# Transposes and first keys as full-array products, an unstrided gate product, and new planner durations in an attention-plus-GLU kernel

## The chip, the cores and the metric

The kernel runs on one core of one Trainium2 chip. The metric is the device time of the whole program in microseconds, the median of several runs. The program before takes 753.09 us (three runs, 751.25 to 753.7).

## What is computed

One sequence of 2048 tokens of width 512 goes through two branches that share their input, and a per-token gate mixes the two results. All inputs are bf16.

```python
# x: [1, 2048, 512]; 32 heads of width 16; F = 1376
def _A_ref(x, wqkv, wo):
    qkv = transpose((x @ wqkv).reshape(B, S, 3, H, Dh), 2, 0, 3, 1, 4)
    q, k, v = qkv[0], qkv[1], qkv[2]
    scores = einsum("bhqd,bhkd->bhqk", q, k) * (Dh ** -0.5)
    p = softmax(scores, axis=-1)
    o = einsum("bhqk,bhkd->bhqd", p, v)
    return transpose(o, 0, 2, 1, 3).reshape(B, S, D) @ wo

def _B_ref(x, w_gate, w_up, w_down):
    return ((x @ w_gate) * (x @ w_up)) @ w_down

g = sigmoid((x * gate_w).sum(-1, keepdims=True))
out = g * _A_ref(A_x, A_wqkv, A_wo) + (1 - g) * _B_ref(A_x, ...)
```

## The kernel before

**Tiles.** x is kept transposed: `xT(kt, lo, hi)` is the 128 features of tile `kt` by the tokens lo to hi. The 2048 tokens are four chunks of 512. A score block is 128 keys by 512 queries of one head: one bank of PSUM (128 x 512 f32). There are 32 rounds `m` (four query chunks, four groups of eight heads, two halves of a group), and each round has 16 key tiles by four heads, so 64 blocks a round and 2048 in all. The array is used as two row groups of 64 rows by four column groups of 32: a "pack" is four matmuls of 64x32 weights and 512 moving columns on one row group, and packs on row groups 0 and 1 run at the same time. In the planner these are the resources `pe0` and `pe1`.

**Exponentials.** Most blocks go from PSUM through ScalarE (ACT, line 1284, two banks to an instruction as a rule) into cells of the tile `PT`. About 550 blocks go through VectorE instead (line 1348): the score is turned into the bits of a bf16, and three shifted copies of it are made (line 1300 on GpSimd, line 1301 on VectorE), which are multiplied with four scaled versions of V (line 728 makes those). So a block of ACT costs one cell and one set of weighted sums, and one of VectorE four.

**Weighted sums.** `pv_pack` (line 1635) multiplies cells with V, whose tiles have a column of ones for the denominators. The last round (m = 31) uses all 128 rows for a product, and forms its denominators with a second product (line 1646). Normalising goes over DMAs (`den`, `rscr`, `rb`), in the last round over ACT (lines 1873 and 1874), then come the last products (lines 1858 and 1882) and the output.

**Fills.** Everything else that TensorE does is a "fill" that the planner puts between score and sum packs: transposing x (`mk_x`, line 580: products of pieces of x with an identity), q, k and v (`mk_q`, `mk_k`, `mk_v`), the gate logits (`mk_gate`, line 764), the GLU (`mk_ug`, `mk_d`) and the output projection (`mk_wo`). All but x and the gate go through `tile4` (line 544). A fill that is not `wide` does its packs on one row group and then the other half of its rows on the other; a `wide` one takes both row groups at once. Each fill has a bank, which VectorE (ACT for two pieces of the first chunk) copies out: line 606 for x, 622 for keys, 738 for v, 679 for q. ACT makes the first q itself, masked, in two instructions (line 697).

**Order.** Nothing is scheduled on the chip. While the program is built, an event-driven planner runs through the whole kernel with assumed durations and writes down for each engine a fixed order, with semaphore waits between engines; an engine then works its list in order, so that an instruction that has to wait holds up all that stands behind it in that list. The assumed durations and policy are the constants at the head of `_build`:

- `PEC` a pack, `PEL` the time until its result can be used, `PSW` a change between the two array shapes, `LEAD`; `a_cad`, `A_LAT`, `d_cad`, `D_LAT`, `p_cad`, `P_LAT` the same for ACT, VectorE and GpSimd
- `PH`: before this time, packs are taken to last twice as long
- `NF0`, `NF`: how many fills may be open at a time, before and after the first `U0` score blocks
- `KF`: how many of the upper four banks a score block for VectorE leaves free while no fill is open
- `WIDE0`: which of the first fills are wide (before: none)

Scores for ACT use banks 0 to 3, all else banks 4 to 7. Score packs come first in `pe_policy`, then sums and fills. At the start x arrives by DMA in five pieces (line 427), followed by weights.

Of the kernel before, what the change touches and what calls it, by code (L numbers as in the profile page):

```python
# [179 lines left out]
def _build(nc, A_x, A_wqkv, A_wo, W_gate, W_up, W_down, gate_w, out):  # L180
# [25 lines left out]
    NH = 2  # L206
    VT = 33 * H // 2
    INF = 1e9
    PEC, PSW, PEL, LEAD = 0.2165, 0.108, 0.41, 0.05
    DTH = 1.2  # L210
    CQ = 3
    VN = 1000
# [8 lines left out]
    AHEAD = 80  # L221
    LOOK = 200
    NF = 1
    NF0 = 3
    U0 = 100
    PB = 4
    PH = 10.5
    VD = 11
    CD = 6
    PL = 8  # L230
# [3 lines left out]
    AB = 4  # L234
    DB = 4
    BURST = 0
    WIDE0 = False
    AW = 0.2
    KF = 1

    def a_cad(n):
        return 0.053 + 0.4267 * n

    A_LAT = 0.17

    def d_cad(n):
        return 0.068 + n / 960.0
# [1 line left out]
    def d_fast(n):  # L249
        return 0.068 + n / 3840.0  # L250

    D_LAT = 0.12

    def p_cad(n):
        return 0.157 + n / 1200.0

    P_LAT = 0.1

    x2 = A_x.rearrange("b s d -> (b s) d")
    out2 = out.rearrange("b s d -> (b s) d")  # L260
# [2 lines left out]
    with ExitStack() as stack:  # L263
# [170 lines left out]
        def xn(ch, tt):  # L434
            return PT[:, xs_first[ch] + tt, :].bitcast(BF16)
# [102 lines left out]
        }  # L538

        def tile4(pe, r, bank, w, lhs, rhs, s0, s1):  # L540
            o = None
            q = slice(0, 128) if r is None else slice(64 * r, 64 * r + 64)
            for i in range((w + 31) // 32):
                o = pe.matmul(  # L544
                    ps[32 * i : min(w, 32 * i + 32), bank, :],
                    lhs(32 * i, min(w, 32 * i + 32))[q],
                    rhs[q],
                    start=s0,
                    stop=s1,
                    tile_position=(64 * (r or 0), 32 * i),  # L550
                    skip_group_check=True,
                )
            return o
# [20 lines left out]
        def mk_x(ch, kt):  # L574
            def pk(pe, bank, rg, s0, s1):
                o_ = None
                q = slice(64 * rg, 64 * rg + 64)
                for tt in range(4):
                    for i in range(4):
                        o_ = pe.matmul(  # L580
                            ps[32 * i : 32 * i + 32, bank, tt * 128 + 64 * rg : tt * 128 + 64 * rg + 64],
                            xn(ch, tt)[q, kt * 128 + 32 * i : kt * 128 + 32 * i + 32],
                            idt[q, q],
                            start=True,
                            stop=True,
                            tile_position=(64 * rg, 32 * i),
                            skip_group_check=True,
                        )
                return o_

            def evac(bank, last):
                def after(o):
                    ev_x[ch, kt] = o
                    release(banks[bank], [o])
                    done_with(("xn", ch), last)

                if ch == 0 and kt % 2:
                    aq_small.append(
                        (0.48, [last], lambda a: a.activation(xT(kt, 0, 512), ps[:, bank, :], ACT.Identity), after)
                    )  # L600
                    return
                dve_job(
                    0,
                    d_cad(512),
                    lambda: [last],
                    lambda v: v.tensor_copy(xT(kt, ch * 512, (ch + 1) * 512), ps[:, bank, :]),  # L606
                    after,
                )

            return _Fill("x", [pk], lambda: d_xn[ch] + [o_id], evac, 0)  # L610

        def mk_k(b, ch):
            def evac(bank, last):
# [144 lines left out]
        def mk_gate():  # L758
            def pk(kt):
                def f(pe, bank, rg, s0, s1):  # L760
                    o_ = None
                    q = slice(64 * rg, 64 * rg + 64)
                    for ch in range(NCH):
                        o_ = pe.matmul(  # L764
                            ps[32 * ch : 32 * ch + 32, bank, :],
                            gwr[q, kt, :],
                            xT(kt, ch * 512, (ch + 1) * 512)[q].rearrange("q (t p) -> q p t", p=128),
                            start=s0,
                            stop=s1,
                            tile_position=(64 * rg, 32 * ch),  # L770
                            skip_group_check=True,
                        )
                    return o_

                return f

            def evac(bank, last):
# [21 lines left out]
                            allow_slow_non_contiguous=True,  # L799
                        )  # L800

                dve_job(2, d_cad(512), lambda: [last], lambda v: v.tensor_copy(grow, ps[:, bank, :]), after)

            def gate2(e1):
                def a1(e2):
# [893 lines left out]
        def fill_issue(t, fu, r, deps):  # L1699
# [3 lines left out]
            g = f.packs[f.pos % n]  # L1703
            own = []
            if f.wide:
                d = to_wide() + {"gate": 0.5, "x": 0.07}.get(f.name, PEC)
                s0, s1 = f.pos == 0, f.pos == n - 1
                o = issue_pe(t, (0, 1), d, PEL - PEC, lambda pe: g(pe, bank, None, s0, s1), deps, "pe_f")
                tot = n
            else:  # L1710
                if f.pos == n:
                    own = [f.last]
                s0, s1 = f.pos == 0, f.pos == 2 * n - 1
                o = issue_pe(t, (r,), to_small() + PEC, PEL - PEC, lambda pe: g(pe, bank, r, s0, s1), deps, "pe_f", own)
                tot = 2 * n
# [217 lines left out]
```

## Time and profile before

| | |
|---|---|
| runs, median (lowest, highest) | 753.09 us (751.25, 753.7) |
| the profiled execution | 751.66 us |
| its span, first to last instruction | 749.8 us |
| TensorE (PE) busy, instructions | 731.3 us, 22327 matmuls |
| ScalarE (ACT) busy | 706.2 us |
| VectorE (DVE) busy | 646.7 us |
| GpSimd (POOL) busy | 505.6 us |
| mean granted TensorE clock | 0.985 |

A matmul's end is modelled and matmuls overlap, so that PE busy at 98% does not mean that the array is at its limit; the other engines' times are measured. "PEld" is the loading of weights, which runs ahead of the matmuls. The time of an instruction on ACT or VectorE overlaps a little with that of the next. "issue" as the reason of idle time means that the profile shows nothing that the engine waited for.

### The profile page before, as it was taken

The numbers are of one execution on the slowest core, as the hardware profiler recorded it, in microseconds if no ns is written. First come the engines' busy times: TensorE is split into PE (matmuls) and PEld (weight loads), VectorE is DVE, ScalarE is ACT, GpSimd is POOL, SyncE is SP. The second block draws the span as 40 slices with busy tenths as digits, with TensorE's granted clock in tenths as the row PEclk, the third lists the DMA queues.
The fourth block names the chain that finished last, engine by engine and source line by source line (L and its number), as shares of the span: only waits on it lengthen the run. The fifth ranks groups of instructions, "written<-read, shape, count | busy, mean of one in ns | idle before, by whom it ended". The sixth has DMA issues, their size and how long they took to land.

```text
span 749.8 us, 49215 instructions
## 1 busy us (share of the span) xinstructions
PE 731.3 (98%) x22327; PEld 367.9 (49%) x22328; DVE 646.7 (86%) x1266; ACT 706.2 (94%) x764; POOL 505.6 (67%) x549
## 2 busy tenths in 40 slices
PE   6999999999999999999999999999999999999996
PEld 4554454555444555545455544445545554444432
DVE  3576599999989999989989988998999888999975
ACT  3699699999998999999999999999999999999985
POOL 1135486878675877878778786786777658585752
PEclk7699999999999999999999999999999999999999
DMA  8200012122005121110512111014221200010100
GB/s 248 65 9 5 9 34 56 43 60 59 9 13 123 39 68 51 52 29 10 118 37 65 51 58 37 16 36 98 55 47 58 65 14 23 8 30 4 28 11 30
DMA packets 77633, 35.01 MB, mean 47 GB/s; under 512 B 60784, under 2 KB 74480, under 8 KB 77424
## 3 DMA queue, kind: packets, MB, share of 16 engines
q1 hardware_dynamic: 76624, 31.47, 17.1%
q8 instruction: 175, 2.87, 1.6%
q10 hardware_dynamic: 800, 0.39, 0.2%
q14 instruction: 34, 0.28, 0.1%
HBM read 25.23 MB, written 2.35 MB: 37 GB/s over the span
## 4 chain that ended last, share of the span: by engine, by line
PE 95%; DMA 1%; DVE 1%; issue 1%; ACT 0%; SPq 0%
PE ps L1635 37%; PE ps L1189 33%; PE ps L544 22%; PE ps L580 1%; PE ps L764 1%; PE ps L1646 1%; DMA PT<-in_B_w_down_dram 1%; DMA PT<-in_A_x_dram 0%; DVE PT L1348 0%; DMA PT<-in_B_w_up_dram 0%; SPq L416 0%; DVE ost L1891 0%; DVE PT L606 0%; ACT rb L1874 0%; PE ps L1882 0%
## 5 line engine op out<-in xcount | busy, mean ns | idle before, releaser
L1284 ACT ACTIVATE PT<-ps 128x1024 bf16<-128x1024 f32 (+1 forms) x750 | 700.4, 1037 | 24.5 <-PE ps L1189 16.6
L1300 POOL TENSOR_SCALAR PT<-PT 128x1024 int16<-128x1024 int16 (+1 forms) x500 | 470.0, 968 | 175.1 <-DVE PT L1301 141.8
L1635 PE MATMUL ps<-PT,VV 64*32 64x512 bf16 (+1 forms) x7275 | 547.0, 377 | 1.5 <-issue 0.3
L1189 PE MATMUL ps<-QT,KT 64*32 64x512 bf16 x8192 | 481.8, 381 | 1.1 <-issue 1.0
L544 PE MATMUL ps<-PT 64*32 64x512 bf16 x5696 | 411.4, 383 | 4.5 <-issue 2.2
L1348 DVE TENSOR_SCALAR PT<-ps 128x512 int16<-128x512 f32 x530 | 358.4, 704 | 50.2 <-PE ps L1189 42.0
L1635 PEld LDWEIGHTS ps<-PT,VV 64*32 64x32 bf16 (+1 forms) x7275 | 179.1, 92 | 126.4 <-PE ps L1635 42.0
L1189 PEld LDWEIGHTS ps<-QT,KT 64*32 64x32 bf16 x8192 | 138.0, 89 | 167.4 <-ACT PT L1284 97.1
L544 PEld LDWEIGHTS ps<-PT 64*32 64x32 bf16 x5696 | 139.0, 92 | 57.4 <-PE ps L544 9.9
L1301 DVE TENSOR_SCALAR PT<-PT 128x1024 int16<-128x1024 int16 (+1 forms) x442 | 152.0, 409 | 0.5
L728 POOL TENSOR_SCALAR VV<-VV 128x528 bf16<-128x528 bf16 x20 | 12.6, 635 | 46.9 <-DVE VV L728 42.8
L544 PE MATMUL ps<-wo,OT 64*32 64x512 bf16 x480 | 36.2, 378 | 0.1
L897 DVE CAST usb<-ps 128x512 bf16<-128x512 f32 (+1 forms) x44 | 30.0, 681 | 1.4 <-PE ps L544 1.4
L912 DVE TENSOR_TENSOR PT<-ps,usb 128x512 bf16<-128x512 f32 (+1 forms) x44 | 29.8, 679 | 1.0 <-PE ps L544 1.0
L1544 POOL TENSOR_TENSOR OT<-oraw,rb 128x512 bf16<-128x512 f32 x16 | 20.5, 1280 | 6.3 <-DMA rb<-rscr 3.5
L1566 DVE COPY oraw<-ps 128x512 f32<-128x512 f32 x31 | 21.2, 684 | 1.0 <-PE ps L1635 0.8
L622 DVE CAST KT<-ps 128x512 bf16<-128x512 f32 x16 | 11.6, 727 | 9.1 <-PE ps L544 8.9
L738 DVE CAST VV<-ps 128x512 bf16<-128x512 f32 x16 | 10.9, 690 | 8.5 <-PE ps L544 8.5
L606 DVE CAST PT<-ps 128x512 bf16<-128x512 f32 x14 | 9.1, 686 | 9.0 <-PE ps L580 9.0
L544 PEld LDWEIGHTS ps<-wo,OT 64*32 64x32 bf16 x480 | 11.5, 91 | 6.7 <-PE ps L544 1.6
L961 DVE TENSOR_SCALAR bsb<-ps,omg 128x512 bf16<-128x512 f32 x16 | 11.8, 738 | 3.2 <-PE ps L544 3.2
L580 PE MATMUL ps<-idt,PT 64*32 64x64 bf16 x512 | 10.5, 220 | 4.0 <-issue 2.2
(45 smaller groups left out, 97.5 us busy)
## 6 DMA issues: line engine op xcount, KB each, us to landing
PT<-in_B_w_up_dram SPq DMA_DIRECT2D x40, 128.0 KB, 3.1
PT<-in_B_w_gate_dram SPq DMA_DIRECT2D x40, 128.0 KB, 3.1
PT<-in_B_w_down_dram SPq DMA_DIRECT2D x20, 256.0 KB, 2.9
rb<-rscr SPq DMA_DIRECT2D x15, 256.0 KB
out_dram<-ost SPq DMA_DIRECT2D x16, 128.0 KB, 1.9
QT<-QR SPq DMA_DIRECT2D x124, 16.0 KB, 2.0
oraw<-oraw SPq DMA_DIRECT2D x60, 32.0 KB, 2.1
PT<-in_A_x_dram SPq DMA_DIRECT2D x3, 512.0 KB, 9.0
```

Of the source, the lines that this page charges most:

```text
L544: o = pe.matmul(ps[32 * i : min(w, 32 * i + 32), bank, :], lhs(32 * i, min(w, 32 * i + 32))[q], rhs[q], start=s0, stop=s1, tile_position=( ...
L580: o_ = pe.matmul(ps[32 * i : 32 * i + 32, bank, tt * 128 + 64 * rg : tt * 128 + 64 * rg + 64], xn(ch, tt)[q, kt * 128 + 32 * i : kt * 128 ...
L897: lambda v: v.tensor_copy(usb[0:w, n % 2, :], ps[0:w, bank, :]),
L912: lambda v: v.tensor_tensor(hT[0:w, f, :], ps[0:w, bank, :], usb[0:w, n % 2, :], ALU.mult),
L1189: o_ = pe.matmul(ps[32 * i_ : 32 * i_ + 32, x, :], KT[64 * r : 64 * r + 64, b, kt * 128 + 32 * i_ : kt * 128 + 32 * i_ + 32], QT[64 * r : ...
L1284: lambda a: a.activation(span(PT, cs).bitcast(BF16), span(ps, bs), ACT.Exp, scale=ESC),
L1300: return lambda e: e.tensor_scalar(span(PT, ds), span(PT, cs), 1.0, float(SH[k]), ALU.mult, ALU.add)
L1301: return lambda e: e.tensor_single_scalar(span(PT, ds), span(PT, cs), float(SH[k]), ALU.add)
L1348: lambda v: v.tensor_scalar(span(PT, cs), span(ps, bs), IOFF, 0.0, ALU.add, ALU.max),
L1544: lambda g: g.tensor_tensor(OT[:, pair % 6, :], oraw[:, 0, :], rb[:, :], ALU.mult),
L1566: lambda v: v.tensor_copy(oraw[:, p, :], ps[:, bank, :]),
L1635: o_ = pe.matmul(ps[32 * j : 32 * j + 32, ob, :], v_ap(k, kt, 8 * b + 2 * j + p, p)[rows], PT[rows, cell, :].bitcast(BF16), start=f0, stop ...
```

## The change

Six things are edited; the order of all work is planned anew with them.

1. x is transposed with full-array products: four of 128x128 for a piece (`mk_x`) in place of 32 of 64x64, with `wide=True`.
2. `WIDE0` goes from `False` to `"k"`: the first four key products (`mk_k(0, ch)`) are wide, and `tile4` makes one 128x128 by 512 product where it made four of 32 columns on each row group.
3. The gate product reads x in its stored order; the copy out of PSUM (line 802) does the reordering that the product's strided read did.
4. The planner's durations change; the last line gives a wide transposition `XC` in place of 0.07.
5. `PH` goes from 10.5 to 0, so that no packs are planned at double length.
6. `NF0` goes from 3 to 2 and `KF` from 1 to 0.

```diff
-    PEC, PSW, PEL, LEAD = 0.2165, 0.108, 0.41, 0.05
+    PEC, PSW, PEL, LEAD = 0.2155, 0.13, 0.437, 0.05
...
-    NF0 = 3
+    NF0 = 2
...
-    PH = 10.5
+    PH = 0.0
...
-    WIDE0 = False
+    WIDE0 = "k"
+    XC = 0.26
     AW = 0.2
-    KF = 1
+    KF = 0
 
     def a_cad(n):
-        return 0.053 + 0.4267 * n
+        return 0.058 + 0.4267 * n
...
-    D_LAT = 0.12
+    D_LAT = 0.15
...
-    P_LAT = 0.1
+    P_LAT = 0.12
...
         def tile4(pe, r, bank, w, lhs, rhs, s0, s1):
+            if r is None:
+                return pe.matmul(ps[0:w, bank, :], lhs(0, w), rhs, start=s0, stop=s1, skip_group_check=True)
             o = None
-            q = slice(0, 128) if r is None else slice(64 * r, 64 * r + 64)
+            q = slice(64 * r, 64 * r + 64)
...
         def mk_x(ch, kt):
             def pk(pe, bank, rg, s0, s1):
                 o_ = None
-                q = slice(64 * rg, 64 * rg + 64)
                 for tt in range(4):
-                    for i in range(4):
-                        o_ = pe.matmul(
-                            ps[32 * i : 32 * i + 32, bank, tt * 128 + 64 * rg : tt * 128 + 64 * rg + 64],
-                            xn(ch, tt)[q, kt * 128 + 32 * i : kt * 128 + 32 * i + 32],
-                            idt[q, q],
-                            start=True,
-                            stop=True,
-                            tile_position=(64 * rg, 32 * i),
-                            skip_group_check=True,
-                        )
+                    o_ = pe.matmul(
+                        ps[:, bank, tt * 128 : tt * 128 + 128],
+                        xn(ch, tt)[:, kt * 128 : kt * 128 + 128],
+                        idt[:],
+                        start=True,
+                        stop=True,
+                        skip_group_check=True,
+                    )
                 return o_
...
-            return _Fill("x", [pk], lambda: d_xn[ch] + [o_id], evac, 0)
+            return _Fill("x", [pk], lambda: d_xn[ch] + [o_id], evac, 0, wide=True)
...
                             gwr[q, kt, :],
-                            xT(kt, ch * 512, (ch + 1) * 512)[q].rearrange("q (t p) -> q p t", p=128),
+                            xT(kt, ch * 512, (ch + 1) * 512)[q],
...
-                dve_job(2, d_cad(512), lambda: [last], lambda v: v.tensor_copy(grow, ps[:, bank, :]), after)
+                dve_job(2, d_cad(512), lambda: [last], lambda v: v.tensor_copy(grow.rearrange("q (p t) -> q p t", t=4), ps[:, bank, :].rearrange("q (t p) -> q p t", p=128)), after)
...
         for f_ in fills:
-            f_.wide = f_.wide or WIDE0
+            f_.wide = f_.wide or f_.name in WIDE0
...
-                d = to_wide() + {"gate": 0.5, "x": 0.07}.get(f.name, PEC)
+                d = to_wide() + (XC if f.name == "x" else PEC)
```

More of the change, by code (lines that the diff above doesn't have):

```diff
@@ L549, in tile4 @@
                     stop=s1,
-                    tile_position=(64 * (r or 0), 32 * i),
+                    tile_position=(64 * r, 32 * i),
                     skip_group_check=True,
```

## The prediction

> **What bounds the kernel now.** I read the page first, then the busy time by stage, then the list of ACT in order of time wherever a stage showed ACT idle.
>
> ```profile
> span 749.8 us, 49215 instructions
> PEclk7699999999999999999999999999999999999999
> L1284 ACT ACTIVATE PT<-ps 128x1024 bf16<-128x1024 f32 (+1 forms) x750 | 700.4, 1037 | 24.5 <-PE ps L1189 16.6
> ```
>
> ```profile
> core 0: us, PE busy (x) PEld busy (x) DVE busy (x) ACT busy (x) POOL busy (x), PEclk, DMA share, GB/s
> 0.00:31.89 31.89, 23.93 (x792) 14.95 (x800) 13.12 (x28) 12.74 (x15) 2.73 (x12) 0.68 0.69 183
> 31.89:75.00 43.11, 42.86 (x1433) 22.59 (x1424) 30.21 (x65) 42.80 (x47) 18.82 (x27) 1.00 0.03 6
> 75.00:86.00 11.00, 11.00 (x144) 4.85 (x128) 3.66 (x6) 5.46 (x5) 3.00 (x2) 1.00 0.01 1
> 86.00:225.00 139.00, 138.21 (x4397) 70.89 (x4398) 127.64 (x248) 137.67 (x150) 106.08 (x115) 1.00 0.16 38
> 225.00:250.00 25.00, 23.59 (x756) 11.55 (x744) 23.56 (x49) 22.97 (x26) 16.41 (x18) 1.00 0.46 97
> 250.00:715.00 465.00, 463.42 (x14316) 232.97 (x14320) 427.71 (x833) 462.13 (x497) 344.66 (x363) 1.00 0.18 44
> 715.00:749.80 34.80, 28.26 (x541) 10.11 (x530) 20.82 (x41) 22.42 (x30) 13.87 (x16) 0.97 0.07 21
> ```
>
> Length less ACT's busy time gives ACT's idle by stage: 19.15, 0.31, 5.54, 1.33, 2.03, 2.87 and 12.38 us, 43.6 in all. Where the bulk of the blocks is worked, ACT is idle under 1% of the time, so the exponentials set the pace: the span is ACT's busy time, 706.2, plus these 43.6. PE's 98% in the page is overlap of modelled ends. The change is therefore priced by what it does to ACT's work and to its three large idle stages: the head, the gate at 75 to 86 us, and the tail.
>
> **The head: what ACT waits for.** ACT in order of time:
>
> ```profile
> 12.39 1.27 ACT L697 ACTIVATE QT<-ps,mask 128x512 bf16<-128x512 f32 x2 [5.16 <-PE ps L544]
> 14.67 1.94 ACT L1284 ACTIVATE PT<-ps 128x1536 bf16<-128x1536 f32 x2 [1.01 <-PE ps L1189]
> 19.23 1.94 ACT L1284 ACTIVATE PT<-ps 128x1024 bf16<-128x1024 f32 x2 [2.62 <-PE ps L1189]
> 23.62 1.02 ACT L1284 ACTIVATE PT<-ps 128x1024 bf16<-128x1024 f32 x1 [2.46 <-PE ps L1189]
> 31.89 28.79 ACT L1284 ACTIVATE PT<-ps 128x1024 bf16<-128x1024 f32 x31 [0.31 <-PE ps L1189]
> ```
>
> The first block goes to ACT at 14.67 and ACT is full only from 31.89. TensorE's weight loads and windows of that time tell why:
>
> ```profile
> 11.93 0.12 PEld L544 LDWEIGHTS ps<-PT 64*32 64x32 bf16 x9 [2.03 <-issue]
> 17.14 0.71 PEld L580 LDWEIGHTS ps<-idt,PT 64*32 64x32 bf16 x58 [2.37 <-issue]
> 21.42 0.10 PEld L544 LDWEIGHTS ps<-PT 64*32 64x32 bf16 x2 [1.87 <-issue]
> ```
>
> ```profile
> 0.90:11.90 11.00, 7.73 (x222) 4.96 (x223) 2.60 (x11) 2.48 (x3) 2.53 (x8) 0.84 0.96 285
> 11.90:17.10 5.20, 2.67 (x128) 1.65 (x127) 3.08 (x5) 3.21 (x4) 0.00 (x0) 0.70 0.85 228
> 17.10:21.40 4.30, 3.06 (x128) 1.61 (x128) 2.58 (x4) 1.94 (x2) 0.00 (x0) 0.50 0.87 181
> 21.40:31.40 10.00, 9.98 (x298) 6.28 (x306) 4.78 (x8) 4.95 (x5) 0.00 (x0) 0.52 0.34 74
> ```
>
> ```profile
> q8 instruction: 175, 2.87, 1.6%
> ```
>
> PE stops three times for about 2 us with nothing to wait for. Between two stops lie 128 matmuls with 128 weight loads, 256 instructions; all 2 x 22328 of them in 256s are 174.4, and the instruction queue moved 175 packets. So a stop is the arrival of the next 256 instructions, and in the head, where small products are used up quickly, nothing covers it. The other thing is the clock: 0.50 to 0.52 through 17.1 to 31.4.
>
> Built, the changed program puts 108 matmuls before its first score product and before puts 312 there; the 223rd, where the first stop came, now lies behind twelve score blocks. So the first stop leaves the path of the first q, and the transposes' other two go.
>
> The Trainium skill ("Runtime: NRT & Kernel Launch", "Instruction fetch mechanics") says that crossing a block of instructions is mostly hidden; by it these stops would have another cause and stay, which is rival 1. The rows show 6.3 us that nothing hides here.
>
> What the change does to the first block, step by step:
>
> ```profile
> 0.99 2.74 PE L483 MATMUL ps<-idz 128*128 128x128 bf16 x24 [0.99 <-DVE mask L487]
> 4.88 1.69 PE L580 MATMUL ps<-idt,PT 64*32 64x64 bf16 x128 [1.15 <-DMA PT<-in_A_x_dram]
> 7.33 1.91 PE L544 MATMUL ps<-PT 64*32 64x512 bf16 x32 [0.76 <-DVE PT L606]
> 13.18 1.88 DVE L606 CAST PT<-ps 128x512 bf16<-128x512 f32 x3
> PT<-in_A_x_dram SPq DMA_DIRECT2D x3, 512.0 KB, 9.0
> 2.29 2.26 SPq L427 DMA_DIRECT2D PT<-in_A_x_dram  x3
> ```
>
> A 128x128 product takes 0.114 us; 16 are 0.9 to 1.8 us by the clock, against 1.69 now, so transposing is not itself faster; four products now finish a piece, so the copies start sooner, by an estimated 0.35 us, and q starts near 6.95 (now 7.33). But q, not wide, is now cut up: four packs on one row group, the wide keys, eight transposes of chunk 1, two packs, a piece of x, one pack, two pieces (the second of chunk 2), the last pack. Chunk 2 is the second of the three loads issued from 2.29 on, near 2.85, and takes the median 9.0: it lands near 11.85. A pack or wide product is 0.2155 us at full clock (four sum packs of the last round below: 723.82 to 724.03, and so on) and 0.43 at half; a change of array shape is 0.1 (724.03 + 0.2155 to 724.35). At full clock throughout, q ends at 12.4, behind chunk 2; with half clock until 11.0 as now, at 13.5. Then the same 1.27 of masked copies and 1.01 to the first exponential: 14.8 to 15.9. I take 15.5, 0.8 later than now.
>
> After that it goes better. The next four blocks wait for copies on VectorE: its q copy stands ahead of two copies of 0.63 each that free banks for the transposes before the second batch of scores: second group near 18.2 (now 19.23). Gaps I take: 0.75, 0.5, 1.5 (56 matmuls of v are 14 packs, 1.5 to 3 us, and there the stop falls), then 1.0 in all. Idle until full: 15.5 less 3.75 (table load, two x copies, masks) is 11.75, plus 3.75 makes 15.5, against 19.15: a gain of 3.6. Bounds: 13.0 with all at full clock (gain 6.1), 21.7 with half clock and a stop uncovered in each gap (loss 2.6). The 17 changes of shape in the head, 1.7 us, are within these; before has one.
>
> The Trainium skill ("TensorE: Matmul & The Clock Gate", "Part 1: The HAM clock gate") has the clock full after one busy window of about 3.4 us. By that the head would reach the 6.1; the row 21.40:31.40 shows PE busy 9.98 of 10 us at 0.52, so I don't count on it (rival 3).
>
> **The gate.**
>
> ```profile
> 80.13 1.27 ACT L1284 ACTIVATE PT<-ps 128x1024 bf16<-128x1024 f32 x1 [2.22 <-PE ps L1189]
> 83.90 1.02 ACT L1284 ACTIVATE PT<-ps 128x1024 bf16<-128x1024 f32 x1 [2.50 <-remote]
> L764 PE MATMUL ps<-PT,gwr x32: 1020/1106/1589, 75.0 to 83.6; 64*32 64x512 bf16 x32
> L544 PE MATMUL ps<-PT 64*32 64x512 bf16 x5696 | 411.4, 383 | 4.5 <-issue 2.2
> ```
>
> Same tile, weights and length as line 544, yet 1106 ns and not 383; only the order in which x is read differs. The score packs queue behind it and ACT idles 5.54. Unstrided, eight packs cost 0.86 us, less than the slack that PE has elsewhere. I count a gain of 5.4; bounds 0 (rival) and 5.5. The copy that now reorders runs once, on VectorE, busy 3.66 of 11.00 us in this stage; even at twice the 0.63 of such a copy it is covered, and without that cover it is 0.6 us.
>
> **ACT's work and VectorE's.** Counted in the built programs, ACT does 1498 blocks and did 1500 (0.467 us each by the page's 700.4): 0.9 less; four more groups of three banks and one, 1.94 in place of the 1.87 of two twos: 0.3 more. Net gain 0.6. VectorE gets two blocks.
>
> **The tail.**
>
> ```profile
> 723.82 0.39 PE L1635 MATMUL ps<-PT,VV 128*32 128x512 bf16 x4
> 724.03 0.39 PE L1646 MATMUL ps<-PT,VV 128*32 128x512 bf16 x4
> 724.35 0.83 PE L1189 MATMUL ps<-QT,KT 64*32 64x512 bf16 x20
> 724.86 13.77 ACT L1284 ACTIVATE PT<-ps 128x1024 bf16<-128x1024 f32 x14 [2.85 <-PE ps L1189]
> 741.10 0.28 ACT L1873 ACTIVATE oraw<-ps 128x128 f32<-128x128 f32 x1 [2.47 <-PE ps L1646]
> ```
>
> Now eight sum packs in a row (0.431 each with its denominators) hold up the scores, 2.85 us, and eight follow the last score (2.47 after the last exponential). In the new order ten packs are spread between scores and 18 follow the last one: ten more, 4.4 us longer at the end, against 2.85 and the 0.7 by which the 14 exponentials exceed 14 x 0.934 (700.4 over 750) gained. I count a loss of 0.8; bounds a gain of 3 and a loss of 4.4.
>
> **Everything else** (new planner durations, `KF`, `PH`): 5.9 us of idle in 86 to 715 and 0.31 before. It can at most go; a stall like 225 to 250 (2.03) could come twice more, 4 us. With nothing to choose by, 0. Fills run later: with 512 blocks left, 1088 of their matmuls remain and before 868, 55 packs or 5.9 us, caught up by 128 left. Their cover is PE's slack; without it they cost those 5.9.
>
> **Sum:** -3.6 - 5.4 - 0.6 + 0.8 = -8.8, span 741.0. Its execution took 751.66, 1.86 more than the span, and the median of the runs is another 1.4 higher; I add 1.86 and half of the 1.4: 743.6.
>
> **Rivals.**
> 1. The head gives nothing: the stops come with the bytes, or q behind chunk 2 costs as much as they did. For it: the first block comes later by my own sum. Against: the three stops are tied to instruction counts. 743.6 + 3.6 = 747.2. Chance 0.18.
> 2. The half clock outlasts the head, and the program is slower. Place: the first rounds, where the plan (`PH` = 0) no longer reckons with it, and full-array pieces wait for VectorE's copies. Price: from 32 blocks' worth of the new order, 114 packs, four ACT blocks need 14.25, 3.07 us at half clock against 1.87 of ACT: 0.39 us lost per us. With the last masks a bit later (first block 16.5, idle 12.75) up to 60 us: 12.75 + 0.39 x 44 = 29.9 of idle against 19.15, so 10.8 lost, 5.2 gained elsewhere: 758. It decides from about 46 us on. Against: the clock came up by 31.4 under the present, thinner start. Chance 0.1.
> 3. Full clock early (741.1), and fewer stalls in the bulk, as the durations fit better (down to 735.2). For it: 31 exponentials in 28.79 us (0.925 each) against 0.934 on average; the Trainium skill's rule on the clock would give the first half of it. Chance 0.18.
> 4. The gate's reading order is not what makes it slow: 743.6 + 5.4 = 749.0. Against: the two rows above. Chance 0.04.
>
> The forecast has 0.5. The range 736 to 751 leaves out rival 2 and the ends of 3; the likeliest case alone spans 740 to 747. Under 0.3% (2.3 us) can't be told from no change, so faster means below 750.8: the forecast, rivals 1 and 3 nearly whole, most of 4, less the unknown of the bulk: 0.82; same 0.08; slower 0.1.
>
> **What would show it.** Head: ACT idle to its first full stretch near 15.5; no stop of 2 us on PE before the first exponential; that exponential at 14.8 to 15.9. Gate: line 764 at about 0.38 us each and no ACT gap over 0.5 there. Tail: 18 sum packs in a row, the logarithm 6 to 7 us after the last exponential. I am wrong if the head's idle is 19 or more, or ACT's idle between 86 and 715 grows by more than 3.

## The result, and the profile after

The changed kernel takes 740.71 us (median of four runs, 739.29 to 743.21); the kernel before, on the same chip, 753.39 us (751.25 to 753.94). The ratio is 0.984 with a 95% interval of 0.981 to 0.987. A second set on another chip gave 743.07 us (six runs) against 751.38, ratio 0.988 [0.985, 0.991]. So the gain lies between 8 and 13 us; forecast were 743.6 and a gain of 8.8 of the span.

The profiled execution took 740.79 us with a span of 737.8, 12.0 less than before. The page of the changed kernel, lines that answer to those quoted of before:

```profile
span 737.8 us, 48084 instructions
PEclk9999999999999999999999999999999999999998
q8 instruction: 170, 2.79, 1.5%
L1284 ACT ACTIVATE PT<-ps 128x1024 bf16<-128x1024 f32 (+1 forms) x749 | 696.2, 1041 | 10.6 <-PE ps L1189 6.5
```

The clock row has lost the 7 and the 6 at its start, and ends in an 8 because the clock falls at 732 us, in the tail. ACT's exponentials have lost 4.2 us of busy time (700.4 before). Where the rest went is read from the busy time by stage, cut at the same times as before (columns: stage, length, then busy time of PE, PEld, DVE, ACT and POOL, granted clock, DMA share, GB/s):

```profile
0.00:31.89 31.89, 28.89 (x532) 15.31 (x536) 18.92 (x43) 18.01 (x21) 7.10 (x19) 1.00 0.72 182
31.89:75.00 43.11, 43.01 (x1368) 22.12 (x1356) 33.06 (x69) 42.95 (x48) 23.22 (x28) 1.00 0.03 8
75.00:86.00 11.00, 10.98 (x328) 5.38 (x312) 10.48 (x22) 10.95 (x14) 8.52 (x9) 1.00 0.18 42
86.00:225.00 139.00, 138.55 (x4372) 74.23 (x4364) 127.31 (x252) 138.25 (x151) 101.97 (x107) 1.00 0.16 39
225.00:250.00 25.00, 23.52 (x772) 12.06 (x756) 20.56 (x38) 23.25 (x26) 17.61 (x18) 1.00 0.35 75
250.00:715.00 465.00, 459.43 (x14212) 242.84 (x14200) 425.24 (x809) 459.32 (x496) 349.00 (x373) 1.00 0.18 44
715.00:737.80 22.80, 16.68 (x260) 5.95 (x256) 9.03 (x29) 9.21 (x16) 3.33 (x3) 0.88 0.10 30
```

Length less ACT's busy time, against before:

| | before | after | difference | forecast |
|---|---|---|---|---|
| head, to 31.89 | 19.15 | 13.88 | -5.27 | -3.6 |
| 75 to 86 (gate) | 5.54 | 0.05 | -5.49 | -5.4 |
| 31.89 to 75 | 0.31 | 0.16 | -0.15 | 0 |
| 86 to 715 | 6.23 | 8.18 | +1.95 | 0 |
| tail, from 715 | 12.38 | 13.59 | +1.21 | +0.8 |
| ACT busy | 706.2 | 701.95 | -4.2 | -0.6 |
| span | 749.8 | 737.8 | -12.0 | -8.8 |

ACT of the changed kernel in order of time (start, length, what ran, and in brackets the idle time before it and its cause), head, gate and tail:

```profile
14.15 1.27 ACT L697 ACTIVATE QT<-ps,mask 128x512 bf16<-128x512 f32 x2 [7.02 <-PE ps L547]
16.15 1.94 ACT L1284 ACTIVATE PT<-ps 128x1536 bf16<-128x1536 f32 x2 [0.73 <-PE ps L1189]
18.40 1.94 ACT L1284 ACTIVATE PT<-ps 128x1536 bf16<-128x1536 f32 x2 [0.31 <-PE ps L1189]
20.84 1.94 ACT L1284 ACTIVATE PT<-ps 128x1536 bf16<-128x1536 f32 x2 [0.51 <-PE ps L1189]
23.01 1.94 ACT L1284 ACTIVATE PT<-ps 128x1536 bf16<-128x1536 f32 x2 [0.23 <-PE ps L1189]
25.25 9.51 ACT L1284 ACTIVATE PT<-ps 128x1536 bf16<-128x1536 f32 x10 [0.29 <-PE ps L1189]
...
63.43 16.88 ACT L1284 ACTIVATE PT<-ps 128x1024 bf16<-128x1024 f32 x18
...
659.26 62.94 ACT L1284 ACTIVATE PT<-ps 128x1024 bf16<-128x1024 f32 x68
728.77 0.28 ACT L1873 ACTIVATE oraw<-ps 128x128 f32<-128x128 f32 x1 [6.57 <-PE ps L1646]
```

The first exponential comes later than before (16.15 against 14.67), but from there to the end of the stage at 31.89 no gap is over 0.51 us, where before had 2.62 and 2.46; the gate stage, now inside the row that starts at 63.43, has no gap; the wait before the logarithm has grown from 2.47 to 6.57. The gate's rows by line:

```profile
L764 PE MATMUL ps<-PT,gwr 64*32 64x512 bf16 x32 | 2.4, 377 | 0.0
L802 DVE COPY PT<-ps 128x512 f32<-128x512 f32 x1 | 0.7, 680 | 0.0
```

1106 ns a product (the median; the mean was 1189) have become 377, and the copy that now reorders took 0.68 us. The head in PEld's list and then in PE's, in order of time; line 543 is now the wide product of `tile4` and line 547 its narrow one:

```profile
9.05 0.13 PEld L543 LDWEIGHTS ps<-PT 128*128 128x128 bf16 x2 [0.84 <-issue]
```

```profile
9.05 1.89 PE L543 MATMUL ps<-PT 128*128 128x512 bf16 x4
14.27 1.04 PE L543 MATMUL ps<-PT 128*128 128x512 bf16 x4
```

0.84 us is the longest stop without a cause in the head; the 2 us stops are gone. And four wide products of one shape took 1.89 us at 9.05 and 1.04 us at 14.27: half clock, then full. The granted clock of the windows says 1.00 for both, since the trace's first clock event stands at 12.1 us; before it the clock has to be read from the products. From 12.1 to 732 us the clock never fell, while before it fell back at 14 us for 17 us.

### The profile page after: what moved, and what is told of

It reads as the page before. It is cut to its first block, busy times and chain, and to the rows that moved or that the text cites. A ratio compares the mean times of both kernels' runs of the same rounds, so it can differ in the third digit from the quotient of the medians.

```text
span 737.8 us, 48084 instructions
## 1 busy us (share of the span) xinstructions
PE 721.1 (98%) x21780; PEld 377.9 (51%) x21780; DVE 644.6 (87%) x1256; ACT 701.9 (95%) x763; POOL 510.8 (69%) x554
## 3 DMA queue, kind: packets, MB, share of 16 engines
q8 instruction: 170, 2.79, 1.5%
## 4 chain that ended last, share of the span: by engine, by line
PE 90%; DMA 3%; ACT 2%; DVE 2%; SPq 2%; issue 1%; POOL 0%; ACTq 0%; DVEq 0%; POOLq 0%
PE ps L1189 31%; PE ps L1635 29%; PE ps L547 27%; ACT PT L1284 2%; SPq L417 2%; PE ps L1646 1%; DVE PT L1348 1%; DMA rb<-rscr 1%; PE ps L581 1%; DMA PT<-in_B_w_up_dram 1%; DMA den<-oraw 1%; PE ps L543 1%; DMA PT<-in_B_w_down_dram 0%; DMA PT<-in_A_x_dram 0%; DVE ost L1891 0%
## 5 line engine op out<-in xcount | busy, mean ns | idle before, releaser
L1300 POOL TENSOR_SCALAR PT<-PT 128x1024 int16<-128x1024 int16 (+1 forms) x505 | 475.0, 969 | 154.1 <-DVE PT L1301 128.5
L1189 PE MATMUL ps<-QT,KT 64*32 64x512 bf16 x8192 | 472.2, 379 | 1.5 <-ACT PT L1284 0.6
L547 PE MATMUL ps<-PT 64*32 64x512 bf16 x5568 | 406.4, 378 | 4.4 <-DMA PT<-in_B_w_up_dram 1.2
L1635 PEld LDWEIGHTS ps<-PT,VV 64*32 64x32 bf16 (+1 forms) x7284 | 184.2, 92 | 105.7 <-PE ps L1635 16.7
L1189 PEld LDWEIGHTS ps<-QT,KT 64*32 64x32 bf16 x8192 | 135.5, 89 | 159.4 <-ACT PT L1284 97.6
L1301 DVE TENSOR_SCALAR PT<-PT 128x1024 int16<-128x1024 int16 (+1 forms) x426 | 150.1, 417 | 0.3
L679 DVE TENSOR_SCALAR QR<-ps 128x512 bf16<-128x512 f32 x16 | 10.8, 672 | 0.4 <-PE ps L547 0.3
```

What stands on the lines that cost most here:

```text
L547: o = pe.matmul(ps[32 * i : min(w, 32 * i + 32), bank, :], lhs(32 * i, min(w, 32 * i + 32))[q], rhs[q], start=s0, stop=s1, tile_position=( ...
L1189: o_ = pe.matmul(ps[32 * i_ : 32 * i_ + 32, x, :], KT[64 * r : 64 * r + 64, b, kt * 128 + 32 * i_ : kt * 128 + 32 * i_ + 32], QT[64 * r : ...
L1300: return lambda e: e.tensor_scalar(span(PT, ds), span(PT, cs), 1.0, float(SH[k]), ALU.mult, ALU.add)
L1301: return lambda e: e.tensor_single_scalar(span(PT, ds), span(PT, cs), float(SH[k]), ALU.add)
L1635: o_ = pe.matmul(ps[32 * j : 32 * j + 32, ob, :], v_ap(k, kt, 8 * b + 2 * j + p, p)[rows], PT[rows, cell, :].bitcast(BF16), start=f0, stop ...
```

## The experiments

Eleven kernels and the change once more, in three sets, each set on one chip beside the kernel before. "Before" was 752.28, 752.33 and 751.38 us at the median in the three sets.

**1. The gate alone, and the change without it.** The first is the kernel before with the gate's edit alone, the second the changed kernel with the gate's edit undone. Each leaves the order of all work as it was.

```diff
 # gate alone: on the kernel before; the change without it: reversed, on the changed kernel
-    xT(kt, ch * 512, (ch + 1) * 512)[q].rearrange("q (t p) -> q p t", p=128),
+    xT(kt, ch * 512, (ch + 1) * 512)[q],
...
-    v.tensor_copy(grow, ps[:, bank, :])
+    v.tensor_copy(grow.rearrange("q (p t) -> q p t", t=4),
+                  ps[:, bank, :].rearrange("q (t p) -> q p t", p=128))
```

> The kernel before with the unstrided gate product and the reordering copy alone; the order of all engines is unchanged. Theory (the score packs queue behind the strided gate matmuls, and ACT's 5.54 us of idle there is lost for good): line 764 falls from 1106 to about 380 ns, ACT's idle between 75 and 86 us goes to under 0.5, and the time falls by 5.0 to 5.5 us, to about 748. Rival A (ACT's idle there is made good later, since something else sets the end): the gap goes but the time falls by less than 2 us. Rival B (the order of reading is not the cause): line 764 stays near 1100 ns.

> The changed kernel with the strided gate product put back; the order of all engines is unchanged. Theory: line 764 near 1100 ns, ACT idle of 5 to 6 us where the gate runs (68 to 78 us), time 740.7 + 5.5 = about 746. Rival A: under 742.5.

The gate alone: 745.08 us, ratio 0.990 [0.988, 0.992], a gain of 7.2. The change without it: 748.2 us (ten runs), ratio 0.995 [0.992, 0.997]. ACT in order of time, the gate alone and then the change without it:

```profile
65.76 22.51 ACT L1284 ACTIVATE PT<-ps 128x1024 bf16<-128x1024 f32 x24
```

```profile
72.56 1.11 ACT L1284 ACTIVATE PT<-ps 128x1024 bf16<-128x1024 f32 x1 [2.22 <-remote]
75.14 1.02 ACT L1284 ACTIVATE PT<-ps 128x1024 bf16<-128x1024 f32 x1 [1.48 <-PE ps L1189]
78.45 8.48 ACT L1284 ACTIVATE PT<-ps 128x1024 bf16<-128x1024 f32 x9 [2.28 <-remote]
```

The gaps come and go with the reading order of x alone, with 1166 ns a product on average where it is strided in the second pair. Since the orders are equal, instruction can be held against instruction. From the 54th to the 80th of ACT's instructions the gate alone moves from 1.17 us behind the kernel before to 5.83 ahead: 7.0 us. The change without it falls 6.8 us behind the changed kernel there. ACT's idle time shows only 5.4 to 6.0 of it. The rest stands in its busy time: between those two instructions ACT is busy 1.4 us less with the gate alone (25.9 to 24.5), and 0.8 us more in the change without it. In the kernel before, two exponentials there took longer than the usual 1.02, the one at 74.87 with 1.77 and the one at 80.13 with 1.27, which makes 1.0 us; why they did was not looked into. The remainder fits that an exponential that starts after a gap doesn't overlap the one before it.

**2. The head's parts alone, and the change with the old durations.** The first is the change without gate and durations, the second the change without durations. The planner gives both the same order.

```diff
 # the change with the old durations; the head's parts alone also have the strided gate
-    PEC, PSW, PEL, LEAD = 0.2155, 0.13, 0.437, 0.05
+    PEC, PSW, PEL, LEAD = 0.2165, 0.108, 0.41, 0.05
...
-        return 0.058 + 0.4267 * n
+        return 0.053 + 0.4267 * n
...
-    D_LAT = 0.15
+    D_LAT = 0.12
...
-    P_LAT = 0.12
+    P_LAT = 0.1
```

> The kernel before with the full-array transposes and keys, XC, PH = 0, NF0 = 2 and KF = 0, but with the strided gate and the former durations; its order is that of the run with the former durations. Theory (the head is worth 5.3 us by itself: no stop of 2 us in front of the scores, full clock from 11.6 us on): ACT idle up to 31.89 us falls from 19.15 to about 14, time about 748. Rival E (the head's gain depends on the durations): idle there above 17. Against the run with the former durations and the unstrided gate it should be 5.5 us slower, a third measure of the gate.

> The changed kernel planned with the former PEC, PSW, PEL, a_cad, D_LAT and P_LAT; wide transposes and keys, unstrided gate, PH, NF0 and KF as changed. ACT's busy time fell by 4.2 us with the change where its count of blocks explains 0.9. Theory C (durations that fit the chip better leave fewer short waits inside ACT's stretches): ACT busy for the exponentials goes back up from 0.465 to 0.467 us a block, some 3 us, and the time to about 744. Rival D (the new durations do nothing, one order is as good as another): within 2 us of 740.7, with the per-block time not tied to the durations.

The head's parts alone: 748.77 us, ratio 0.995 [0.993, 0.998], a gain of 3.5. With the 7.2 of the gate alone that makes 10.7, between the 8.3 and the 12.7 of the change's two sets. The idle time of the head itself fell by more than 3.5, to 13.70 us; but between 31.89 and 86 us, where the strided gate runs, ACT idles 9.39 us in that order where the kernel before has 5.85 (the clock was at half there for 3.41 us, from 76.5 on). With the old durations: 741.68 us, ratio 0.985 [0.983, 0.988], within the spread of the changed kernel. It differs from the head's parts alone by the gate's edit only, so the 7.1 us between them are a third measure of the gate. The new durations are worth nothing that these runs can tell: ACT has 1498 blocks in place of 1502, and the exponential of two banks takes 0.929 us on average in place of 0.932 (686.5 over 739 and 678.6 over 728), but ACT idles 5.68 us between 250 and 715 in place of 2.27, and 1.75 between 225 and 250 in place of 0.00.

The two profiles gave something else. PE's wide products and ACT's first exponential, old durations and then the head's parts alone:

```profile
7.44 1.04 PE L543 MATMUL ps<-PT 128*128 128x512 bf16 x4
...
13.53 1.94 ACT L1284 ACTIVATE PT<-ps 128x1536 bf16<-128x1536 f32 x2 [0.73 <-PE ps L1189]
```

```profile
9.07 1.89 PE L543 MATMUL ps<-PT 128*128 128x512 bf16 x4
...
15.99 1.94 ACT L1284 ACTIVATE PT<-ps 128x1536 bf16<-128x1536 f32 x2 [0.73 <-PE ps L1189]
```

One order, one set of instructions in the head, and the first exponential differs by 2.46 us. The clock had become full at 4.25 us in the one execution and at 11.65 in the other, and the 2.46 us stay between the two, instruction by instruction, until the gate's products start (67.4 and 69.9 us).

**3. More instructions ahead of the first scores.** My forecast had put the 2 us stops down to counts of instructions. Two kernels put about as many matmuls ahead of the first score product as the first stop wanted (223 and 240, where the changed kernel has 108), with the order of all else unchanged: one by 139 warm-up products of 8 columns for the 24 of 128, the other by cutting each transposing product into four.

```diff
 # more instructions
-        for _ in range(24):
+        for _ in range(139):
...
-    pe.matmul(ps[:, 7, 0:128], idz[:], idz[:], start=True, stop=True, skip_group_check=True)
+    pe.matmul(ps[:, 7, 0:8], idz[:], idz[:, 0:8], start=True, stop=True, skip_group_check=True)
```

```diff
 # narrow transposes
-    o_ = pe.matmul(ps[:, bank, tt * 128 : tt * 128 + 128],
-                   xn(ch, tt)[:, kt * 128 : kt * 128 + 128], idt[:], start=True, stop=True, ...)
+    for i in range(4):
+        o_ = pe.matmul(ps[32 * i : 32 * i + 32, bank, tt * 128 : tt * 128 + 128],
+                       xn(ch, tt)[:, kt * 128 + 32 * i : kt * 128 + 32 * i + 32], idt[:],
+                       start=True, stop=True, tile_position=(0, 32 * i), ...)
```

> The changed kernel with 139 warm-up matmuls of 8 columns in place of 24 of 128, in the idle time before x arrives; all else in the same order. 223 matmuls now precede the first score product, the number behind which the kernel before had its first stop. Theory (a stop is the fetch of the next 256 instructions, uncovered where products are short): TensorE's weight loads show an idle time of 1 to 2 us with no cause between 12 and 17 us, and the first exponential moves from 16.15 to between 17 and 18.2; time up by 0.5 to 2 us, to 741 to 743. Rival F (the stops belong to the transposes of 64 columns or to the half clock): no such idle time, first exponential within 0.3 us of 16.15.

> The changed kernel with each 128x128 transposing product issued as four on 128 rows by 32 columns side by side; same plan, same order, 192 matmuls more in the head, so that 240 precede the first score product. Theory: a stop of about 2 us before the first score, another within the next 128 matmuls, first exponential near 18, ACT's idle up to 31.89 us from 13.9 to 16 to 18, time 743 to 745. Rival F: no stop; the four side by side take no longer than the one, and the time stays within 1.5 us of 740.7.

More instructions: 738.55 us, ratio 0.983 [0.978, 0.988]. Narrow transposes: 737.23 us, ratio 0.980 [0.976, 0.983]. Neither is slower than the change. PE, PEld and ACT of the first:

```profile
0.99 3.87 PE L484 MATMUL ps<-idz 128*128 128x8 bf16 x139 [0.99 <-DVE mask L488]
...
9.14 0.13 PEld L543 LDWEIGHTS ps<-PT 128*128 128x128 bf16 x2 [0.84 <-issue]
...
16.22 1.94 ACT L1284 ACTIVATE PT<-ps 128x1536 bf16<-128x1536 f32 x2 [0.73 <-PE ps L1189]
```

The 223rd matmul now lies ahead of the first score as in the kernel before, no stop is longer than the 0.84 that the changed kernel has as well, and the first exponential stays where it was (16.22, 16.15). So the count alone doesn't make a stop of 2 us. In the narrow transposes the first exponential came at 18.51, but there the clock became full only at 17.17; at half clock up to that point, it had no stop over 0.84 us either, so the half clock doesn't make the stops.

The packets of the instruction queue in the traces show what does. In the kernel before, the first three, of 16 KB each, ended at 10.55, 15.83 and 20.15 us, and the three stops ended 1.39, 1.31 and 1.26 us behind them; with the gate alone, whose stops are of 2.10, 2.79 and 2.15 us, it is 1.50, 1.44 and 1.38. In the other twelve executions the first three packets ended at least 1.8 us ahead of the weight loads at the counts 223, 350 and 478 (in the change 5.0, 2.0 and 2.1). The matmuls between two stops ran for 2.8 and 2.4 us. From the 95th matmul to its first stop the kernel before took 4.4 us; the kernel with more instructions took 12.0 over the same stretch, with no stop in it over 0.84. So a stop is a wait for the next instructions, as forecast, but it comes where the matmuls ahead are used up faster than the next packet arrives. The two kernels above had the count of the kernel before and not its pace.

**4. The first q wide too.** It is the piece that waits longest in the head, and the change leaves it narrow.

```diff
-    WIDE0 = "k"
+    WIDE0 = "kq"
```

> The changed kernel with the first q product also made full-array, so that it is done in one piece and no longer waits behind the transposes of chunk 2. Theory (the first exponential is late because q is cut up and ends behind chunk 2, which lands near 11.85): first exponential at 12 to 13.5 instead of 16.15, ACT idle up to 31.89 us down by 2 to 4 us, time 737 to 739. Rival G (what ACT does not get early it gets later; the first scores only move the wait to the keys of chunk 1): first exponential earlier, but ACT idle up to 31.89 still above 13 and the time within 1.5 us of 740.7.

740.42 us, ratio 0.985 [0.982, 0.988]: no gain over the change that the runs can tell. ACT's first exponential and the stage 250 to 715:

```profile
9.93 1.94 ACT L1284 ACTIVATE PT<-ps 128x1536 bf16<-128x1536 f32 x2 [1.03 <-PE ps L1189]
```

```profile
250.00:715.00 465.00, 461.35 (x14076) 244.82 (x14076) 422.68 (x811) 457.97 (x495) 345.50 (x360) 1.00 0.17 43
```

The first exponential comes 6.2 us sooner, and the head idles 4.6 us less. A part of that is the clock, full from 3.65 us here: against the change with the old durations, whose clock was full at 4.25, it is 3.6 us sooner and idles 2.1 less. And the order planned from there has ACT do 1505 blocks where the change has 1498, some 3.3 us at 0.465 each, and ACT idles 1.35 us more in this stage (7.03). That takes back about as much as the head gave. The other stages differ too, and the profiled execution as a whole is 1.5 us shorter than that of the change.

**5. Wide transposes without the wide keys.** Gate and wide x on the kernel before, with narrow keys, `KF`, `NF0`, `PH` and the durations as they were.

```diff
 # the changed kernel, but
-    WIDE0 = "k"
+    WIDE0 = ""
...
-    KF = 0
+    KF = 1
 # and NF0 = 3, PH = 10.5, old durations
```

> The run with the former durations, with the keys narrow again and NF0, PH and KF as before: so the kernel before with full-array transposes and the unstrided gate alone. 116 matmuls precede the first score. Theory (the head gains by fewer instructions, and the transposes are nearly all of these): ACT idle up to 31.89 us at 11 to 14 as with the keys wide, time 740 to 743, against 745.1 of the gate alone. Rival H (wide keys, NF0, PH and KF carry the head's gain): idle there 16 or more, time 744 to 747.

750.2 us (ten runs), ratio 0.997 [0.995, 0.999]: 5 us slower than the gate alone. Its list of ACT, and busy time by stage:

```profile
13.32 1.94 ACT L1284 ACTIVATE PT<-ps 128x1536 bf16<-128x1536 f32 x2 [0.84 <-PE ps L1189]
15.48 1.94 ACT L1284 ACTIVATE PT<-ps 128x1536 bf16<-128x1536 f32 x2 [0.23 <-PE ps L1189]
...
48.85 1.94 ACT L1284 ACTIVATE PT<-ps 128x1536 bf16<-128x1536 f32 x2 [0.23 <-PE ps L1189]
51.03 9.38 ACT L1284 ACTIVATE PT<-ps 128x1024 bf16<-128x1024 f32 x10 [0.24 <-PE ps L1189]
```

```profile
31.89:66.00 34.11, 34.04 (x1088) 18.21 (x1072) 28.21 (x59) 31.80 (x35) 22.22 (x29) 1.00 0.03 7
```

The head is better than the change's (idle 12.01), but the planned order falls into groups of three banks and one, with 0.2 to 0.5 us of wait before each, up to 51 us, and ACT does 1509 blocks (1500 with the gate alone) and is busy 6.4 us longer. So neither theory held: the idle time is the first one's, the time is beyond the rival's. Which of `KF`, `NF0`, `PH` and the keys leads out of it wasn't tried.

**6. What is left in head and tail.** Four kernels on one chip: the change again; twelve warm-up products more and twelve dummy products behind the first chunk's transposes, to keep TensorE busy; sum packs ahead of scores in the last round, while the planner counts a backlog; and both.

```diff
 # keep warm
-        for _ in range(24):
+        for _ in range(36):
...
-                0.11,
+                0.11 * 24 / 36,
...
+                if ch == 0 and kt == KD - 1:
+                    for _ in range(12):
+                        pe.matmul(ps[:, 3, 0:128], idz[:], idz[:], start=True, stop=True, ...)
```

```diff
 # last round, at the head of the policy
+            if m == last_m and backlog(t) > 0.3:
+                g = pv_go(t, r, False)
+                if g or g is None:
+                    return bool(g)
```

> The changed kernel once more, as the mark that the next three are held against on the same chip. All theories: 739 to 743 us at the median, ratio to the kernel before 0.981 to 0.987, first exponential at 16.15 us if the TensorE clock becomes full at 12.1 us again; if the clock becomes full earlier or later, the first exponential moves with it.

> Twelve warm-up products more at the start and twelve dummy products behind chunk 0's transposition; the order of all else is that of the changed kernel. Theory (the head waits for the full TensorE clock): clock full by 7.8 us, first exponential at 13.5 to 14.5 us, ScalarE's idle time up to 31.89 us at 11 to 12 us instead of 13.88, and the time 2.0 to 2.5 us below the changed kernel. Rival (the moment of the full clock doesn't hang on how busy TensorE is, or the first exponential is bound by the arrival of chunk 2): clock full at about 12 us again, first exponential 16.0 to 16.6, time within 1 us of the changed kernel.

> In the last round sum packs go ahead of scores while the planner counts a backlog, so 5 packs stand behind the last score instead of 18. Theory (the last logarithm waits for packs that could have run earlier): its wait falls from 6.57 to 2 to 3 us, gaps between the last exponentials grow by under 1.5 us in all, and the time falls by 2 to 4 us. Rival (TensorE is the bound of the last round, so that the wait is only moved): the log's wait falls by as much, ScalarE's gaps before it grow by 3 to 4 us, and the time is within 1 us of the changed kernel.

> Both edits together. If head and tail are two separate waits on ScalarE's path, the gains add: 4 to 6 us below the changed kernel, about 735 to 737 us. If one of the two edits gives nothing by itself, the sum is that of the other alone.

| | median, us | range | ratio to before |
|---|---|---|---|
| the change again | 743.07 | 739.37 to 745.95 | 0.988 [0.985, 0.991] |
| keep warm | 739.36 | 735.39 to 739.82 | 0.982 [0.979, 0.985] |
| last round | 742.9 | 740.19 to 745.21 | 0.988 [0.985, 0.990] |
| both | 738.19 | 735.85 to 744.98 | 0.984 [0.980, 0.988] |

Keep warm did as its theory said, nearly: PE and ACT of it, to be read against 9.05 and 16.15 of the change:

```profile
8.42 1.04 PE L543 MATMUL ps<-PT 128*128 128x512 bf16 x4
...
14.51 1.94 ACT L1287 ACTIVATE PT<-ps 128x1536 bf16<-128x1536 f32 x2 [0.96 <-PE ps L1192]
```

The clock was full at 6.86 us, the first exponential came at 14.51, and ACT idled 12.16 in the head. Against the change again it is ahead by 2.1 us at ACT's 200th instruction; the rest of the 3.7 between the medians is within what stops and drops of the clock later on (last section) do to single executions. Against the first set of the change, a gain in time isn't shown: the ratios to the kernel before, 0.982 and 0.984, have overlapping intervals, and the two profiled executions are within 0.5 us of each other at the end. It is not shown either that the dummies brought the clock up: executions with the head of the change had it full at 11.44, 12.1, 12.6 and 17.27 (first exponential at 16.01, 16.15, 16.41 and 18.32), the two with dummies at 6.86 and 4.26, but a kernel without them also at 4.25.

The last round followed the rival. ACT's tail in it:

```profile
721.33 1.02 ACT L1284 ACTIVATE PT<-ps 128x1024 bf16<-128x1024 f32 x1 [1.58 <-PE ps L1189]
722.65 1.02 ACT L1284 ACTIVATE PT<-ps 128x1024 bf16<-128x1024 f32 x1 [0.29 <-PE ps L1189]
...
734.54 0.28 ACT L1877 ACTIVATE oraw<-ps 128x128 f32<-128x128 f32 x1 [1.99 <-PE ps L1646]
```

The logarithm waits 1.99 us in place of 6.57, and ten gaps ahead of it, 1.58 and nine of 0.23 to 0.36, add up to 4.2. TensorE needs 1.32 us for two score blocks and their sums there (721.33 to 722.65), ACT 1.02. TensorE is the bound of the last round, and the wait is only moved. Both edits together are 1.2 us below keep warm alone, with ranges that overlap: no gain of the last round that the runs can tell.

## Why the prediction was right

The time, 743.6, lies 2.9 above the first median and 0.5 above the second, and the forecast's case, a gain in head and gate, is what happened. Its terms were less good than their sum: the span fell by 12.0 and not by 8.8, since the head and ACT's work gave 1.7 and 3.6 us more than was counted, and idle time between 86 and 715, put at nothing, took 1.95 back. That the second median is within half a microsecond is luck.

**The gate was mis-sized.** -5.4 was read from ACT's idle time, and the idle time did what it said (-5.49), but the gate was worth 6.8 to 7.2 us in three pairs of kernels (7.0 and 6.8 by instructions, 7.2 and 7.1 by times on one chip). The bounds, 0 to 5.5, didn't hold it. An idle column leaves out what a stall does to the length of the instructions beside it. The mechanism was right: line 764 at 377 ns (forecast 0.38), no gap, a copy that hides. The Trainium skill ("SBUF — State Buffer", "Door 1: The DMA port swizzle") adds a likely reason: lines of 16 bytes, with a penalty for each access to a new one. The strided product read elements 256 bytes apart, and its mean of 1166 to 1189 ns against 377 agrees; no run here varied the stride.

**The head: sum near, terms off.** The profile has -5.27, the head's parts alone -3.5 at the median, forecast -3.6. The first exponential came at 16.15, behind the end of its range (14.8 to 15.9), with half clock to 12.1 and not to 11.0. The range's lower end was wrong as well: it had q end behind chunk 2, at 12.4 even with full clock. With full clock from 4.25 (the old durations) q's last products ran from 11.03, the first exponential came at 13.53, and no product waited for chunk 2; the three loads took 7.3 us at the median and not 9.0. The gaps after the first exponential were 1.34 us, forecast 3.75: the dense stretch begins at 25.25. The 1.5 counted for v's products and a stop fell away.

**The stops: the mechanism was right, the condition was not.** No stop of 2 us came before the first exponential, as forecast, and a stop is a wait for the next instructions: the packets in experiment 3 show it. But the forecast placed it by the count of matmuls, and by count alone experiment 3 should have had one. In the kernel before, and with the gate alone, the stops come at the same counts (223, 350 and 478 matmuls); in the other twelve executions the packets are ahead of these counts and no stop comes. The pace decides: with transposes of 32 small products among them, 128 matmuls were used up in 2.4 to 2.8 us. The Trainium skill's "mostly hidden" ("Runtime: NRT & Kernel Launch", "Instruction fetch mechanics") holds for those twelve, and not for the 2 us of the kernel before.

**ACT's work** fell by 4.2, forecast 0.6. The gate's edit alone took 1.6, the two blocks fewer and the four more 3+1 groups the forecast 0.6; some 2 us are left that come with the new durations (0.929 against 0.932 us for 739 exponentials makes 2.3) and are given back as idle time between 250 and 715 (+2.8). Nothing for the durations was right on balance.

**Idle time in the bulk** was the weakest term. It was put at nothing for want of a reason (from 5.9 us; the stages add up to 6.23), with a growth of more than 3 us named as a sign of being wrong. It grew by 1.95 here, but by 7.3 in the profiled execution of the change again, and by 0.4 to 4.1 in six others that share the order up to the last round. The last section has causes for 4.4 of the 7.3.

**The tail** was right: 18 sum packs in a row, a wait of 6.57 (forecast 6 to 7), 1.21 us lost (forecast 0.8, with the ten packs at 4.4 us; 10 x 0.431 is 4.3). Experiment 6 shows why so little: the order of packs there only moves TensorE's bound.

**The rivals.** The first (the head gives nothing) falls with the head's parts alone, whose interval ends below 1; the second (half clock up to 60 us) with the clock, full from 12 us, or 17 at the latest; the fourth with line 764. The third, 741.1 down to 735.2, holds the first median, but not by its mechanism: the clock was full at 12.1 and not early, and the bulk idled more; the head did better than forecast by its shorter gaps. (The 0.925 us an exponential that spoke for it is 0.929 if 28.79 is divided by 31.) The Trainium skill's rule on the clock ("TensorE: Matmul & The Clock Gate", "Part 1: The HAM clock gate") would have had the clock full after one busy window of about 3.4 us; the kernel before has 9.98 us of 10 busy at 0.52, which disagrees. The same section has the window run free of the program's start, and the instants of one head, 11.44, 12.1, 12.6 and 17.27, agree with that.

## What to carry over

Price a stall by how far the same instructions of two kernels with one order move apart, not by the idle column alone: here 0.8 and 1.4 of the gate's 7 us stood in the busy time. Where a planner writes the order anew, a gain at one place (the earlier first exponential of experiment 4) can go into an order that gives more work to the bounding engine; build the order, count that engine's blocks, and test each edit with the order held. In a head of a few us, ask first when the clock becomes full; it moves the head by up to 2.5 us from one execution to the next. And to explain a stop without a cause, look at when the instruction queue's packets end, and not only at how many instructions lie between two stops.

## What the runs showed of the hardware

The runs of the kernels with the changed order spread over 4 to 9 us, and the traces show a cause, which need not be the only one. Near 235 us the order planned with the new durations makes TensorE stop. The chain of waits of the change again, there (start, length, what):

```profile
232.84 1.33 SPq L417
...
234.85 1.88 DMA den<-oraw
...
236.92 0.64 DVE PT L1348
...
237.60 0.40 PE ps L547 x4
```

The SPq rows ahead of the denominators' DMA are four copies of q (`QT<-QR`, 231.61 to 234.80 us) that SyncE issues one behind the other, with weight loads ahead of them. VectorE waits 3.20 us for the denominators with score blocks behind, and TensorE waits 2.75 us for VectorE. In the profiled execution of the change this stop took 1.14 us; in six others of the same planned order 1.69 to 3.19 us. With the old durations and in the kernel before no stop of TensorE there waits for VectorE, and none is over 1 us (0.51 and 0.98). In five of the six executions of this order with a stop above 2 us the clock then falls to half for one window of 3.41 us; in the sixth, both edits with 2.74 us, it doesn't, nor after 2.34 us in the kernel with the wide q. Busy time in that stage, the change again and then the change:

```profile
235.00:240.00 5.00, 2.36 (x48) 0.85 (x56) 2.65 (x6) 1.54 (x2) 2.15 (x3) 0.79 0.27 56
```

```profile
235.00:240.00 5.00, 4.94 (x164) 2.50 (x164) 4.43 (x8) 3.77 (x5) 3.26 (x5) 1.00 0.29 59
```

With the same order, ACT's 220th to 240th instructions fell behind by 2.5 us by this, and by 1.9 more at a second drop (627.0 to 630.41, behind a stop of 1.14 for a weight's DMA). Stop and drop together differ from one execution to the next, so that two single executions of one order can be 2 to 4 us apart for this alone. A version that issues the denominators' DMA ahead of the copies of q, or from another queue, was not tried.
